# Another order for words 331 to pair 10, and seventeen steps on other engines

## The chip, the cores and the metric

The kernel runs on one core of a Trainium2 chip. A core has five engines that each work through their own list of instructions in order: TensorE (PE, with its weight loads PEld), VectorE (DVE), ScalarE (ACT), GpSimd (POOL) and SyncE (SP), which issues nearly all DMAs here. They meet through semaphores alone. The metric is the device time of one execution in microseconds (us); lower is better.

## The reference

Windowed attention in front of a feed-forward block with a SoLU gate, all in float32, with errors held small enough that the large products are taken in high and low parts:

```
scores = q k^T / 8, masked: heads 0-3 a window of 32, heads 4-7 every 4th of 128 back
attn   = softmax(scores);  x = attn v            8 batches x 576 tokens, 8 heads of 64
h      = x @ w_in                                4608 tokens, 512 -> 1024
solu   = h * softmax(h)
ln     = (solu - mean) / sqrt(var + 1e-6) * g_ln
out    = ln @ w_out                              1024 -> 512
```

## The kernel before

**Work.** Attention goes in 32 units (a batch and two heads); the feed-forward block in 36 tiles of 128 tokens. The order of everything is written out by hand as a list of words: a name and a number is one step of one unit or tile. `OPENING` (line 50) holds the words of the first 26 tiles or so, word for word; behind it `pair_words` (line 137) makes the words for pairs of tiles r = 13 to 17. `run` and the loop at line 1006 call one small function for each word, in order, and each function appends its instructions to the lists of the engines it uses. Nothing is moved afterwards: the order of the words *is* the order on each engine, and an engine that waits holds all that stands behind it on that engine, SP's DMA issues too.

**A unit n.** `S` scores on PE (line 311, 40 matmuls, each recorded as two of 64 columns), `mask` and `max` on DVE (329, 340), `sub` on POOL (353), `exp` on ACT (357), `sum` and `inv` on DVE (361, 367), `norm` on DVE or POOL (372), `turn` on DVE (377: the weights are transposed into `pt`), `V` on PE (406: 80 or 92 small matmuls with `pt`), then `xh`/`xf` on ACT (450, 453) and `xl`/`xd` (464, 471, or a DMA) put x into the tiles x_hi and x_lo.

**A tile i.** Tiles 0 to 11 take `ha` to `hd` on PE (485); from tile 12 on two tiles r = 6, 7, ... share seven block products `P1` to `P7` (844) on sums `z`, `hS`, `lS`, `hA`, `lA` (672, 675, 802, 817), whose results ACT and DVE gather (`s` 862, `c` 868). Then `peak` or `pk` (496, 875) and `gate` (520) on DVE, `e` (511) and `var` (536) on ACT, `mid` (centring: DVE 532, or ACT 529), `forth` and `back` (the tile goes to DRAM and comes back with its rows turned), `trA`/`trB` on DVE (592), `thA`/`thB` on ACT (600: high part), `tlA`/`tlB` on POOL or DVE (606: low part), `o` or `oA`, `oB` on PE (615: 24 or 12 matmuls of 512 columns) and `out` (627).

**Which engine.** Tables by number decide for the steps that either of two engines can do:

```
371  eng = nc.gpsimd if n in POOL_NORM else nc.vector
527  if (i in ACT_CENTRE) != (PAIRED <= i < NTILE - 2):   # then centre on ACT, else on DVE
605  on_pool = i < NTILE - 3 and f"tl{'AB'[c]}{i}" not in ON_DVE
```

So for tiles 12 to 33 a tile named in `ACT_CENTRE` is centred on DVE, and one that is not named on ACT.

Of the kernel before, what the change touches and what calls it, by code (L numbers as in the profile page):

```python
# [37 lines left out]
SIGN_BIT = 1 << 15  # L38
PE_MASK = (0, 1, 2, 3, 4, 5, 6, 7, 8, 9)
POOL_SUB = True  # L40
POOL_NORM = (0, 1, 2, 3, 4, 5, 6, 7, 8, 9, 12, 14, 15, 20, 22)
ACT_SCORES = ()
POOL_X = (2, 4, 5, 6, 9)
DVE_LOW = (0, 4, 8, 9, 10, 11, 12, 14, 15)
ACT_CENTRE = (0, 3, 4, 5, 6, 7, 8, 10, 11, 14, 15, 16, 17, 18, 19)
Q_BUFS, V_BUFS, T_BUFS, TH_BUFS, CONV_BUFS = 4, 4, 4, 2, 4
REBIAS = 2.0**-112
TO_ZERO = 2.0**-100
# [73 lines left out]
)  # L122
PAIR_HEAD = "S.u V.y P1.r trB.c xf.y P2.r trA.c s1.r mask.u thB.c "
# [43 lines left out]
WIDE = ()  # L167
AFTER = {}
SHIFT = {}
ON_DVE = ("tlA2", "tlB2", "tlA4", "tlA6", "fc0", "fb1", "fh0", "fa1", "fd1", "fc1", "tlB7", "fh1", "tlA9", "tlB9", "tlA10", "tlA11", "tlA12", "tlB14", "tlA16", "tlB16", "tlB17", "tlB18", "tlA18", "tlA19", "tlB3", "tlB4", "tlB5", "fd0", "tlA5", "tlA7", "fg1", "tlB10", "tlB11", "tlA13", "tlB13", "tlA14", "tlB19", "fe0", "fg0", "tlA8", "tlB15", "tlA17",)  # L170


@with_exitstack
def windowed_attention_then_solu_kernel(
# [159 lines left out]
    def wide(x):  # L334
        return x.unsqueeze(3).broadcast_to([P, 2, NS, WQ])
# [33 lines left out]
    def soft_norm(n):  # L369
        sm, rs = st[n]["sm"], st[n]["rs"]  # L370
        eng = nc.gpsimd if n in POOL_NORM else nc.vector
        eng.tensor_tensor(out=sm, in0=sm, in1=wide(rs), op=ALU.mult)
# [152 lines left out]
    def moe_centre(i):  # L525
        src, dst, mu = ms[i]["t"], ms[i]["t"], ms[i]["mu"]
        if (i in ACT_CENTRE) != (PAIRED <= i < NTILE - 2):
            nc.vector.tensor_scalar(out=mu, in0=mu, scalar1=-1.0 / DF, scalar2=None, op0=ALU.mult)  # L528
# [29 lines left out]
    def part_of_t(name, i):  # L558
        name = f"{name}{i % TH_BUFS}"
        if name in SHIFT and name not in shifted:  # L560
            shifted.add(name)
            moe.tile([P, SHIFT[name]], F32, name=f"before_{name}", bufs=1)
        return moe.tile([P, FT, P], F32R, name=name, bufs=1)
# [38 lines left out]
    def low_t(i, c):  # L602
        if "tl" not in ms[i]:
            ms[i]["tl"] = part_of_t("tl", i)
        on_pool = i < NTILE - 3 and f"tl{'AB'[c]}{i}" not in ON_DVE
        (nc.gpsimd if on_pool else nc.vector).tensor_tensor(  # L606
# [104 lines left out]
    def sums_engine(word):  # L711
        return nc.vector if word in ON_DVE else nc.gpsimd

# [378 lines left out]
```

## Time and profile before

| | |
|---|---|
| three runs, median | 492.19 us (491.38 to 492.32) |
| the profiled execution, its own time | 491.03 us |
| its span, first to last instruction | 489.2 us |
| granted TensorE clock, mean | 1.000 |
| PE busy | 462.2 us, 94% of the span; 6988 matmuls, each with a weight load |
| DVE, ACT, POOL busy | 358.4, 299.6, 263.1 us |

PE is the engine to read: from 37 us on, the page shows it busy for 90% or more of every fortieth of the span but the last. Matmuls are pipelined, so a long matmul's own duration (390 ns) says little; the distance from one start to the next does.

### The profile page before, as it was taken

How to read it: one execution, taken by the hardware profiler on the slowest of the kernel's cores; microseconds unless marked ns; L12 is line 12 of the kernel's file. 1: busy time of each engine (PE TensorE's matmuls, PEld its weight loads, DVE VectorE, ACT ScalarE, POOL GpSimd, SP SyncE). 2: the span in 40 equal slices, each digit the busy share in tenths (PEclk: the TensorE clock that was granted, in tenths of full speed). 3: DMA queues.
4: the chain of work that ended last, by engine and by line, in shares of the span. 5: the costliest groups of instructions: out<-in, count | busy, mean ns of one | idle time of the engine just before them, and what ended most of it. 6: DMA issues, size and time to landing. Idle time of an engine off the chain costs nothing.

```text
span 489.2 us, 16365 instructions
## 1 busy us (share of the span) xinstructions
PE 462.2 (94%) x6988; PEld 373.9 (76%) x6988; DVE 358.4 (73%) x625; ACT 299.6 (61%) x502; POOL 263.1 (54%) x332
## 2 busy tenths in 40 slices
PE   2559999999999999999999999999999999999997
PEld 1346788888887887878778878888888888888885
DVE  1857999868879796879678997788496754445572
ACT  3769898455653445664555544866486666667552
POOL 0344467535352549958862734466576756766420
PEclk9999999999999999999999999999999999999999
DMA  8887766657743374755676855766755545353462
GB/s 302 343 291 271 236 206 189 199 188 247 246 146 108 121 225 119 237 153 162 226 219 168 253 187 193 211 214 213 254 172 161 165 135 166 98 166 120 121 179 78
DMA packets 50760, 94.05 MB, mean 192 GB/s; under 512 B 5632, under 2 KB 25472, under 8 KB 50688
## 3 DMA queue, kind: packets, MB, share of 16 engines
q1 hardware_dynamic: 49968, 92.37, 60.0%
q8 instruction: 54, 0.88, 0.8%
q10 hardware_dynamic: 720, 0.66, 0.4%
q14 instruction: 18, 0.15, 0.1%
HBM read 59.97 MB, written 28.31 MB: 180 GB/s over the span
## 4 chain that ended last, share of the span: by engine, by line
PE 78%; DVE 10%; POOL 4%; ACT 3%; issue 3%; DMA 1%; SPq 0%; DVEq 0%; ACTq 0%; POOLq 0%
PE banks L615 32%; PE banks L844 21%; PE banks L485 10%; PE banks L406 6%; PE banks L311 5%; PE banks L650 2%; DVE mx L340 1%; DVE t L592 1%; DMA packed<-pack 1%; DVE t L520 1%; PE banks L303 1%; DVE low L672 1%; DVE sm L350 1%; DVE tl L606 1%; DVE pt L377 1%
## 5 line engine op out<-in xcount | busy, mean ns | idle before, releaser
L615 PE MATMUL banks<-w_o,th 128*128 128x512 f32 x544 | 169.1, 392 | 0.0
L615 PEld LDWEIGHTS banks<-w_o,th 128*128 128x128 f32 x544 | 101.3, 188 | 21.7 <-DVE w_o L943 0.4
L615 PE MATMUL banks<-w_o,tl 128*128 128x512 f32 x272 | 106.2, 390 | 1.2 <-DVE tl L606 1.2
L606 POOL TENSOR_TENSOR tl<-t,th 128x512 fp32r<-128x512 f32 x35 | 47.1, 1353 | 42.1 <-ACT th L600 42.1
L485 PE MATMUL banks<-w_i,x_hi 128*128 128x512 f32 x192 | 62.1, 405 | 0.0
L615 PEld LDWEIGHTS banks<-w_o,tl 128*128 128x128 f32 x272 | 51.1, 188 | 12.6 <-DVE tl L606 2.0
L600 ACT CAST th<-t 128x512 fp32r<-128x512 f32 x68 | 41.0, 618 | 22.5 <-DVE t L592 19.0
L868 DVE CUSTOM_DVE_ANT_0 t<-banks,t 128x512 f32<-128x512 f32 x36 | 24.5, 682 | 37.3 <-PE banks L844 29.0
L406 PEld LDWEIGHTS banks<-pt,vt 32*64 32x64 f32 x2752 | 35.0, 140 | 14.7 <-issue 8.1
L592 DVE STREAM_TRANSPOSE t<-raw 128x512 f32<-128x512 f32 x68 | 45.3, 689 | 0.5 <-DMA raw<-mid 0.5
L406 PE MATMUL banks<-pt,vt 32*64 32x64 f32 (+3 forms) x2752 | 38.5, 236 | 6.9 <-issue 4.7
L353 POOL TENSOR_TENSOR sm<-sm,mx 128x640 f32<-128x640 f32 x22 | 29.2, 1328 | 28.4 <-DVE mx L340 28.4
L485 PEld LDWEIGHTS banks<-w_i,x_hi 128*128 128x128 f32 x192 | 35.3, 190 | 7.6
L511 ACT ACTIVATE e<-t,nmax 128x1024 f32<-128x1024 f32 x23 | 26.5, 1152 | 22.8 <-DVE nmax L875 22.6
L311 PEld LDWEIGHTS banks<-kt,qt 64*32 64x32 f32 x2560 | 29.5, 110 | 14.2 <-issue 11.4
L627 ACT ACTIVATE ob<-banks,rstd 128x512 f32<-128x512 f32 x35 | 24.0, 686 | 26.0 <-PE banks L615 17.5
L529 ACT ACTIVATE t<-t,mu 128x1024 f32<-128x1024 f32 x25 | 28.8, 1153 | 18.1 <-DVE mu L528 17.6
L536 ACT ACTIVATE e<-t 128x1024 f32<-128x1024 f32 x35 | 37.0, 1056 | 4.3 <-DVE t L532 4.1
L311 PE MATMUL banks<-kt,qt 64*32 64x64 f32 x2560 | 35.5, 235 | 3.5 <-issue 3.5
L485 PE MATMUL banks<-w_i,x_lo 128*128 128x512 f32 x96 | 38.1, 397 | 0.1
L606 DVE TENSOR_TENSOR tl<-t,th 128x512 fp32r<-128x512 f32 x37 | 30.6, 842 | 8.3 <-ACT th L600 6.7
L862 ACT COPY t<-banks 128x512 f32<-128x512 f32 x36 | 21.1, 587 | 24.1 <-PE banks L844 21.2
(161 smaller groups left out, 937.4 us busy)
## 6 DMA issues: line engine op xcount, KB each, us to landing
mid<-t SPq DMA_DIRECT2D x140, 128.0 KB, 2.7
raw<-mid SPq DMA_DIRECT2D x34, 512.0 KB, 4.1
vt<-vw SPq DMA_DIRECT2D x32, 384.0 KB, 4.4
kt<-kT SPq DMA_DIRECT2D x32, 312.0 KB, 4.8
qt<-qT SPq DMA_DIRECT2D x32, 296.0 KB, 5.2
out<-ob SPq DMA_DIRECT2D x35, 256.0 KB, 2.7
x_hi<-x SPq DMA_DIRECT2D x12, 288.0 KB, 3.9
t<-w_in SPq DMA_DIRECT2D x5, 512.0 KB, 6.5
```

The source lines that it names most:

```text
L311: nc.tensor.matmul(out=ps[WIN * c : WIN * c + WIN, h, WQ * i : WQ * i + WQ], lhsT=qt[D * h : D * h + D, q0 : q0 + WIN], rhs=kt[D * h : D * ...
L353: eng.tensor_tensor(out=st[n]["sm"], in0=st[n]["sm"], in1=wide(mx), op=ALU.subtract)
L406: nc.tensor.matmul(out=ps_x[D * h : D * h + D, c, c0 : c0 + k1 - k0], lhsT=vt[WIN * c : WIN * c + WIN, i, D * h : D * h + D], rhs=pt[WIN * ...
L485: nc.tensor.matmul(out=ps_h(i)[:, half], lhsT=a[:, kt, xs], rhs=w_i[:, kt, half, part, :], start=(kt == 0 and k == 0), stop=(kt == KT - 1 ...
L511: nc.scalar.activation(out=e, in_=h, func=AF.Exp, bias=nmax, scale=1.0, accum_out=se)
L529: nc.scalar.activation(out=dst, in_=src, func=AF.Identity, bias=mu, scale=1.0)
L536: nc.scalar.activation(out=e, in_=t, func=AF.Square, accum_out=per_tile(i, "sq"))
L592: nc.vector.transpose(out=turned(i)[:, cut(c)].rearrange("p k (a r) -> p k a r", r=WIN), in_=ms[i]["mv"].rearrange("p (a k s) -> p k a s", ...
L600: nc.scalar.copy(out=ms[i]["th"][:, cut(c)], in_=turned(i)[:, cut(c)])
L606: (nc.gpsimd if on_pool else nc.vector).tensor_tensor(out=ms[i]["tl"][:, cut(c)], in0=turned(i)[:, cut(c)], in1=ms[i]["th"][:, cut(c)].bit ...
L615: nc.tensor.matmul(out=ps_o(i), lhsT=a[:, f, :], rhs=w_o[:, f, part, :], start=(f == 0 and k == 0), stop=(f == FT - 1 and k == 2), skip_gr ...
L844: nc.tensor.matmul(out=banks[:, bank], lhsT=left(pa, kt), rhs=right(pb, kt), start=j in (1, 2, 5) and kt == 0 and k == 0, stop=kt == 1 and ...
```

## The change

It replaces the middle of `OPENING` from word 331 (`S11`, `mask11`, ...) to where the sums of pair 11 are ready (680 words, the same ones in another order; the 330 before and the 497 behind are untouched). The new order comes from a planner that asks for half a microsecond between the end of a step and its use by TensorE. Three tables change with it:

- `POOL_NORM`: units 10, 11, 21, 23, 25 move their `norm` from DVE to POOL, unit 20 from POOL to DVE.
- `ACT_CENTRE`: tiles 9, 16, 17, 18, 19 move their `mid` from DVE to ACT, tiles 6, 8, 20, 21 from ACT to DVE.
- `ON_DVE`: `tlA3` and `tlB6` move from POOL to DVE.

```
-POOL_NORM = (0, 1, 2, 3, 4, 5, 6, 7, 8, 9, 12, 14, 15, 20, 22)
+POOL_NORM = (0, 1, 2, 3, 4, 5, 6, 7, 8, 9, 10, 11, 12, 14, 15, 21, 22, 23, 25)
-ACT_CENTRE = (0, 3, 4, 5, 6, 7, 8, 10, 11, 14, 15, 16, 17, 18, 19)
+ACT_CENTRE = (0, 3, 4, 5, 7, 9, 10, 11, 14, 15, 20, 21)
...
-    "trB2 trA2 back3 out1 e5 gate5 thA2 hc6 mid5 trB3 back4 ha6 S11 mask11 out0 xh8 tlA2 thB2 "
+    "trB2 trA2 back3 out1 e5 gate5 thA2 hc6 mid5 trB3 back4 ha6 var5 thB2 tlA2 max10 q12 S11 "
...
-ON_DVE = (..., "tlB15", "tlA17",)
+ON_DVE = (..., "tlB15", "tlA17", "tlA3", "tlB6",)
```

On PE the words of the stretch stand, before and now (the bars enclose runs of small attention matmuls):

```
before  |S11| hd6 hb6 o2 ha7 hb7 |V9 S12| hc7 hd7 o3 |V10 S13| ha8 hc8 hd8 hb8 o4 |S14 V11| ha9 hc9 o5
        hb9 hd9 |S15 V12| o6 ha10 hb10 hc10 hd10 o7 ha11 |V13 S16| hc11 hb11 |V14| hd11 o8 |V15| o9 P1.6
        |S17| P2.6 P5.6 P6.6 P3.6 P7.6 |S18| P4.6 P2.7 oA10 P1.7 P5.7 oB10 |S19 V16| P6.7 P3.7 P7.7 oA11
        |S20 V17| P4.7 oB11 P2.8 |V18| P1.8 oA12 P6.8 P5.8 |V19| oB12 P7.8 P3.8 |S21| oA13 oB13 |S22| oA14
        P4.8 oB14 P1.9 P5.9 |S23 V20| P2.9 P6.9 P3.9 oA15 P7.9 |S24 V21| P4.9 oB15 P5.10 P1.10 oA16 P2.10
        oB16 |V22 S25| oA17 oB17 P6.10 P3.10 |V23| P7.10 oA18 oB18 P4.10 oA19 oB19
now     |S11| hd6 hb6 |S12| o2 |V9| ha7 hb7 hc7 hd7 |V10 S13| o3 ha8 hc8 hd8 hb8 o4 |V11 S14| hc9 o5
        hd9 ha9 hb9 o6 |S15 V12| hc10 ha10 hb10 hd10 |S16| o7 ha11 |V13| hc11 hd11 |V14| o8 |V15| hb11 o9
        P1.6 |S17| P5.6 P6.6 P2.6 |S18| P3.6 P7.6 oA10 P4.6 oB10 P1.7 P5.7 |V16| P2.7 P6.7 |S19| P3.7 P7.7
        |V17 S20| P4.7 oA11 oB11 P1.8 P2.8 P5.8 |V18 S21| oA12 P6.8 oB12 P7.8 P3.8 |V19| oA13 oB13 |S22|
        P4.8 oA14 |S23 V20| oB14 P1.9 P2.9 P5.9 P6.9 P3.9 P7.9 oA15 oB15 P4.9 P2.10 |S24 V21| P1.10 P5.10
        oA16 oB16 |V22 S25| P6.10 oA17 |V23| P3.10 oB17 P7.10 oA18 oB18 P4.10 oA19 oB19
```

Three places in the built programs (names carry the buffer's number and a running number; the running numbers differ between the two programs). First VectorE ahead of `V15`; `x_lo` is `xl14`, `pt1` is `turn15`. Before:

```order
L471 TENSOR_TENSOR x_lo_89<-banks_90,x_hi_88 128x576
L672 TENSOR_TENSOR mag3_2835<-vt2_2097,more_2361 128x512
L672 TENSOR_TENSOR mag1_2837<-qt3_1807,tp_2120 128x512
L592 STREAM_TRANSPOSE t1_2497<-raw5_2586 128x512
L329 TENSOR_TENSOR sm0_93<-banks_90,packed_83 128x10x64
L340 TENSOR_REDUCE mx_2872<-sm0_93 128x10
L606 TENSOR_TENSOR tl1_2878<-t1_2497,th1_2843 128x512
L377 STREAM_TRANSPOSE pt1_2880<-sm1_94 128x640
```

Now:

```order
L672 TENSOR_TENSOR kt3_1808<-kt3_1808,vt2_1995 128x512
L471 TENSOR_TENSOR x_lo_89<-banks_90,x_hi_88 128x576
L329 TENSOR_TENSOR sm0_93<-banks_90,packed_83 128x10x64
L340 TENSOR_REDUCE mx_2821<-sm0_93 128x10
L471 TENSOR_TENSOR x_lo_89<-banks_90,x_hi_88 128x576
L377 STREAM_TRANSPOSE pt1_2830<-sm1_94 128x640
L606 TENSOR_TENSOR tl1_2834<-t1_2483,th1_2776 128x512
L592 STREAM_TRANSPOSE t1_2483<-raw5_2748 128x512
```

Between `xl14` and `turn15` stood six steps, and none stands there now.

Second, VectorE ahead of `oA17`; `tl1` is the low part that `oA17` reads, `mx` with `sm0` the maximum of unit 24, `sm1` unit 23. Before (the double row at `tl1` is `tlA17` and `tlB17`):

```order
L672 TENSOR_TENSOR vt2_3877<-x_hi_88,vt2_3877 128x256
L531 TENSOR_SCALAR mu_4389<-mu_4389 128x1
L532 TENSOR_SCALAR t3_4136<-t3_4136,mu_4389 128x1024
L361 TENSOR_REDUCE rs_4399<-sm1_94 128x10
L592 STREAM_TRANSPOSE t1_3737<-raw5_4285 128x512 x2
L340 TENSOR_REDUCE mx_4420<-sm0_93 128x10
L592 STREAM_TRANSPOSE t2_4064<-raw4_4375 128x512
L367 RECIPROCAL rs_4399<-rs_4399 128x10
L606 TENSOR_TENSOR tl1_4483<-t1_3737,th1_4402 128x512 x2
```

Now (the first row is `tlA17`, and the second `tl1` row `tlB17`; `mx_4383` is again unit 24):

```order
L606 TENSOR_TENSOR tl1_4251<-t1_3774,th1_4219 128x512
L868 ISA t3_4142,m2_4339<-banks_90,zero_98 128x512
L868 ISA m2_4339 128x1
L875 TENSOR_SCALAR nmax_4341<-m1_4190,m2_4339 128x1
L606 TENSOR_TENSOR tl0_4237<-t0_3718,th0_4152 128x512
L340 TENSOR_REDUCE mx_4365<-sm1_94 128x10
L520 ISA t3_4142,mu_4367<-t3_4142,e_4350 128x1024
L520 ISA mu_4367 128x1
L329 TENSOR_TENSOR sm0_93<-banks_90,packed_83 128x10x64
L340 TENSOR_REDUCE mx_4383<-sm0_93 128x10
L528 TENSOR_SCALAR mu_4367<-mu_4367 128x1
```

`tlA17` stood behind the sum of unit 23 and the maximum of unit 24, and now stands ahead of the gate of tile 19 and of both maxima.

Third, TensorE at `S16` (the row of line 311); before it follows `V13` (the four rows of line 406) in one run of small matmuls:

```order
L485 MATMUL banks_90<-w_i_86,x_hi_88 128x512 x2
L485 MATMUL banks_90<-w_i_86,x_lo_89 128x512
L406 MATMUL banks_90<-pt1_2556,vt1_2177 64x32 x6
L406 MATMUL banks_90<-pt1_2556,vt1_2177 64x64 x24
L406 MATMUL banks_90<-pt1_2556,vt1_2177 64x48 x8
L406 MATMUL banks_90<-pt1_2556,vt1_2177 64x16 x8
L311 MATMUL banks_90<-kt0_2352,qt0_2351 32x64 x40
L485 MATMUL banks_90<-w_i_86,x_hi_88 128x512 x2
```

Now:

```order
L485 MATMUL banks_90<-w_i_86,x_hi_88 128x512 x2
L485 MATMUL banks_90<-w_i_86,x_lo_89 128x512
L311 MATMUL banks_90<-kt0_2383,qt0_2382 32x64 x40
L615 MATMUL banks_90<-w_o_87,th1_2377 128x512 x2
L615 MATMUL banks_90<-w_o_87,tl1_2380 128x512
```

`S16` has become a run of its own between products of 512 columns.

## Rows read from the trace of the kernel before

**Rows 1.** Windows: length, busy PE, PEld, DVE, ACT, POOL, PE clock, DMA share, GB/s.
```profile
100.69:316.59 215.90, 213.11 (x3339) 172.95 (x3339) 177.70 (x294) 119.05 (x201) 121.90 (x154) 1.00 0.61 190
```
**Rows 2.** The two longest waits of PE there: total us, times, longest us.
```profile
PE banks L615 <- DVE tl L606: 1.2, 2, 0.6
PE banks L406 <- DVE pt L377: 0.8, 1, 0.8
```
**Rows 3.** Timeline of PE at `S11`: start us, us, instructions.
```profile
99.92 0.62 PE L485 MATMUL banks<-w_i,x_hi 128*128 128x512 f32 x2
100.37 0.39 PE L485 MATMUL banks<-w_i,x_lo 128*128 128x512 f32 x1
100.69 1.04 PE L311 MATMUL banks<-kt,qt 64*32 64x64 f32 x80
101.66 0.73 PE L485 MATMUL banks<-w_i,x_hi 128*128 128x512 f32 x2
102.23 0.40 PE L485 MATMUL banks<-w_i,x_lo 128*128 128x512 f32 x1
```
**Rows 4.** Timeline of PE: the end of `o8`, and `V15`.
```profile
183.13 0.39 PE L615 MATMUL banks<-w_o,tl 128*128 128x512 f32 x1
184.29 1.08 PE L406 MATMUL banks<-pt,vt 32*64 32x64 f32 x80 [0.77 <-DVE pt L377]
```
**Rows 5.** Timeline of PE: `V12`.
```profile
150.36 0.83 PE L406 MATMUL banks<-pt,vt 32*64 32x32 f32 x56
151.92 0.64 PE L406 MATMUL banks<-pt,vt 32*64 32x64 f32 x36 [0.72 <-issue]
```
**Rows 6.** Timeline of PE: the first matmuls of `oB10`.
```profile
210.11 0.40 PE L615 MATMUL banks<-w_o,th 128*128 128x512 f32 x1
211.09 0.51 PE L615 MATMUL banks<-w_o,tl 128*128 128x512 f32 x1 [0.58 <-DVE tl L606]
211.43 0.40 PE L615 MATMUL banks<-w_o,th 128*128 128x512 f32 x1
```
**Rows 7.** Timeline of PE: the first matmuls of `oA17`.
```profile
291.49 0.73 PE L615 MATMUL banks<-w_o,th 128*128 128x512 f32 x2
292.81 0.50 PE L615 MATMUL banks<-w_o,tl 128*128 128x512 f32 x1 [0.58 <-DVE tl L606]
```
**Rows 8.** Timeline of PE: second and third matmul of `P7.8`.
```profile
242.80 0.39 PE L844 MATMUL banks<-low,w_i 128*128 128x512 f32 x1
243.23 0.50 PE L844 MATMUL banks<-qt,w_i 128*128 128x512 f32 x1
```
**Rows 9.** DMA queues of the page: packets, MB, share of 16 engines.
```profile
q8 instruction: 54, 0.88, 0.8%
```
**Rows 10.** Timeline at 285 us: `gate19` and `lA2.10` on DVE, `sub23` on POOL.
```profile
285.36 1.23 DVE L520 CUSTOM_DVE_ANT_0 t<-t,e 128x1024 f32<-128x1024 f32 x1
...
286.51 1.47 DVE L672 TENSOR_TENSOR vt<-x_hi,vt 128x256 fp32r<-128x256 f32 x1
...
285.40 2.31 POOL L353 TENSOR_TENSOR sm<-sm,mx 128x640 f32<-128x640 f32 x1 [3.34 <-DVE mx L340]
```
**Rows 11.** `sub` on POOL, all 22: duration ns min/median/max.
```profile
L353 POOL TENSOR_TENSOR sm<-sm,mx x22: 1260/1264/2309, 107.3 to 383.5; 128x640 f32<-128x640 f32 x22
```
**Rows 12.** Groups by line: count, busy us, mean ns, idle before.
```profile
L372 DVE TENSOR_TENSOR sm<-sm,rs 128x640 f32<-128x640 f32 x17 | 15.4, 911 | 0.3
L372 POOL TENSOR_TENSOR sm<-sm,rs 128x640 f32<-128x640 f32 x15 | 19.4, 1294 | 30.4 <-DVE rs L367 28.7 <-ACT ob L627 1.6
L532 DVE TENSOR_SCALAR t<-t,mu 128x1024 f32<-128x1024 f32 x11 | 10.6, 965 | 0.4
L529 ACT ACTIVATE t<-t,mu 128x1024 f32<-128x1024 f32 x25 | 28.8, 1153 | 18.1 <-DVE mu L528 17.6 <-POOL tl L606 0.5
L606 DVE TENSOR_TENSOR tl<-t,th 128x512 fp32r<-128x512 f32 x37 | 30.6, 842 | 8.3 <-ACT th L600 6.7 <-issue 1.0 <-ACT th L642 0.7
L606 POOL TENSOR_TENSOR tl<-t,th 128x512 fp32r<-128x512 f32 x35 | 47.1, 1353 | 42.1 <-ACT th L600 42.1
```

More of the change, by code (lines that the diff above doesn't have):

```diff
@@ L169 @@
 SHIFT = {}
-ON_DVE = ("tlA2", "tlB2", "tlA4", "tlA6", "fc0", "fb1", "fh0", "fa1", "fd1", "fc1", "tlB7", "fh1", "tlA9", "tlB9", "tlA10", "tlA11", "tlA12", "tlB14", "tlA16", "tlB16", "tlB17", "tlB18", "tlA18", "tlA19", "tlB3", "tlB4", "tlB5", "fd0", "tlA5", "tlA7", "fg1", "tlB10", "tlB11", "tlA13", "tlB13", "tlA14", "tlB19", "fe0", "fg0", "tlA8", "tlB15", "tlA17",)
+ON_DVE = ("tlA2", "tlB2", "tlA4", "tlA6", "fc0", "fb1", "fh0", "fa1", "fd1", "fc1", "tlB7", "fh1", "tlA9", "tlB9", "tlA10", "tlA11", "tlA12", "tlB14", "tlA16", "tlB16", "tlB17", "tlB18", "tlA18", "tlA19", "tlB3", "tlB4", "tlB5", "fd0", "tlA5", "tlA7", "fg1", "tlB10", "tlB11", "tlA13", "tlB13", "tlA14", "tlB19", "fe0", "fg0", "tlA8", "tlB15", "tlA17", "tlA3", "tlB6",)
 @with_exitstack
```

104 rows, old and new, of the table OPENING are left out of this document.

## The prediction

> **What bounds the kernel now.** I read the windows first. In the changed stretch, 215.90 us long, TensorE is busy for 213.11, at a granted clock of 1.00, which is the 2.4 GHz level; VectorE has 177.70, GpSimd 121.90, ScalarE 119.05 [rows 1]. So TensorE bounds the stretch, its work is the same before and after, and no order can save more than the time in which it issues nothing or issues late. The idle time alone is 215.90 - 213.11 = 2.8 us. PE's waits put names to most of it: 1.2 us in two waits for a low part, 0.8 for a transposed `pt` [rows 2], and 0.72 in the middle of `V12` under "issue", where no semaphore is seen [rows 5].
>
> The busy time hides more, because a matmul is booked with its latency. The distances between starts show it. Inside `ha6` two matmuls take 100.37 - 99.92 = 0.45 us, so 0.227 each; a run of small matmuls starts 0.32 behind the last wide one (0.09 more than the pitch), and behind it the first two wide ones take 102.23 - 101.66 = 0.57, 0.12 more [rows 3]. Each run of attention matmuls so costs 0.2 us for being apart from the others, whatever waits.
>
> **What the waits cost, one by one.** Read from starts, with the pitches just given:
>
> - `V15`: from `o8`'s last matmul to its first, 184.29 - 183.13 = 1.16 instead of 0.32: 0.84 [rows 4]. It waited for `turn15`.
> - `V12`: 56 small matmuls from 150.36, which at `S11`'s rate (0.97 us for 80 [rows 3]) take 0.68; the next starts at 151.92: 0.88 lost, with no producer named [rows 5].
> - `oB10`: 211.09 - 210.11 = 0.98 instead of 0.227, and the one behind starts 0.34 later, 0.11 over the pitch (the price of a restart): 0.86 [rows 6].
> - `oA17`: 292.81 - 291.49 = 1.32 where two matmuls behind small ones take 0.57: 0.75 [rows 7].
> - `P7.8`: 0.43 instead of 0.227, and a restart: 0.31 [rows 8]. Two more products (`P5.7`, `P6.8`) show the restart alone: 0.22.
>
> Together 3.86 us. That is what the new order can give back at most.
>
> **The change, part by part.** *Waits removed.* `turn15`: before, six VectorE steps stand between `xl14` and `turn15`; now none does. `V14`, `xl14` and `turn15` follow each other while `o8`'s 24 matmuls run, 24 x 0.227 = 5.4 us, and a VectorE step of this size takes about 0.9 us [rows 12]. What is late next there is the chain from `V15` to `P5.6` (x copied, `z1`, `z2`, `z4`, `lS12` on GpSimd), which has `hb11`, `o9`, `P1.6` and `S17` beside it; that is as much cover as before. `tlA17`: now ahead of `gate19` and both maxima, and five products (`oA16` and `oB16` among them) and two runs of attention stand between that point of the list and `oA17`; it has several us to spare. `tlB10` stood on VectorE behind `gate13` and now stands ahead of `norm16` and of everything that VectorE does for pair 6. I take these stalls, and those at `P7.8`, `P5.7` and `P6.8`, as gone at their old places (the last three I did not count out); what comes in their stead is the unknown below.
>
> `V12`: the 54 packets of the instruction queue hold 0.88 MB [rows 9], 16 KB each; PE has 13,976 matmuls and weight loads, about 256 to a packet. `S15` and `V12` are 172 small matmuls, 344 instructions, issued within 2 us: here one whole packet lies inside small matmuls, and I read the wait as the next one's arrival. Counted in the new order, only the run `V22 S25` still holds a whole packet, and it did before, without a wait. I take the 0.88 as gone; if it stays, the sum is 0.9 higher.
>
> The Trainium skill speaks against this reading: "Runtime: NRT & Kernel Launch", section "Instruction fetch mechanics", says that fetching is hidden because instructions are dispatched slower than they are filled in. By that rule the wait has another cause and may come back, and the sum would be 1.6 us instead of 2.5. The trace has an "issue" wait with no producer in the middle of `V12`, which is nearer to the fetch.
>
> *Runs added.* `V9 S12`, `V13 S16` and `S19 V16` are split, and `V18` and `S21` are joined; 20 runs become 22. Two more at 0.2 us: +0.4. It could be 0 if the split runs stand where PE waits anyway, and 0.45 by the pitches above.
>
> *Steps on other engines.* Norms: net four fewer on VectorE (4 x 0.91 = 3.6 us) and four more on GpSimd (4 x 1.29 = 5.2). Centrings: five leave VectorE and four come (0.97 against 1.15 on ScalarE, net about 1 us). Low parts: two more on VectorE (1.7 us), two fewer on GpSimd (2.7) [rows 12]. VectorE ends some 3 us lighter of 178, GpSimd 2.5 heavier of 122. None of this is on TensorE's path; the cover is the 0.5 us planned ahead of each use. If the cover fails, a step costs what it is late, plus 0.11.
>
> *Waits added.* This is the unknown part. A step that uses two inputs in SBUF on GpSimd can be stretched by one on VectorE: `sub23` took 2.31 us beside `gate19`, where the median is 1.26 [rows 10, 11], so 1.05 late, and `lA2.10`, which stood ahead of `tlA17` on VectorE, took 1.47 beside `sub23`. Half a microsecond covers half of the 1.05: 1.05 - 0.5 + 0.11 = 0.66 for each use that is hit. Of the waits above, those at `oB10`, `oA17` and `P7.8` have such a step in their chain. If as many are hit again, and half of these stand where only the planned 0.5 is spare, 1.5 x 0.66 = 1.0 us comes back. The bounds: 0 (no use is hit; below 0 is excluded, since PE can't go under its pitch) and 3.9, all that was lost before. I take 1.0, nearer to the lower end, because the waits were of 0.6 to 0.8 us and the spare of 0.5 is most of that.
>
> "SBUF — State Buffer", section "Who interferes with whom" of the Trainium skill, has a stricter form: of a GpSimd step and a VectorE step with two SBUF inputs, the later waits for the whole of the earlier. `sub23` agrees: the gate's 1.23 us and then its own 1.26 from 285.36 end at 287.85, and it ended at 287.71. By that rule the four norms that go to GpSimd raise the number of such meetings; what this would do is the third rival below.
>
> **Sum.** -3.86 + 0.40 + 1.0 = -2.5 us. The profiled execution would go from 491.03 to 488.5; the median of the runs stands 1.16 above that execution, so 492.19 becomes **489.7 us**.
>
> **Rivals.** *All the spare holds.* No use is late: -3.86 + 0.4 = -3.5, 488.7 us. For it: the waits shown are all under 0.9 us. Against it: single steps are stretched by more than 0.5.
>
> *The waits only move.* The spare is a plan's and not a measured one; the old order, too, was written out with every step ahead of its use, and lost 3.86. If new uses lose as much less the 0.4 of the runs, say 3.5, the time stays at 492.2. For it: VectorE is busy for 82% of the stretch. Against it: the old waits stand where the producer was within 0.1 us of its use or behind it, and most uses with half a us were not hit.
>
> *GpSimd's queue is late (slower).* In pairs 7 to 10, `z1` to `z4`, `lS12`, `lS34`, `sub` and now the norms of units 21, 23 and 25 follow each other on GpSimd, and each waits for the one before. If two steps of such a chain are each stretched by 1.05, a product loses 2 x 1.05 - 0.5 + 0.11 = 1.7; with one in each of three pairs, 5.1 us, and the sum is -3.86 + 0.4 + 5.1 = +1.6: 493.8 us. It decides from the point where GpSimd's products wait in three of the four pairs. For it: norms with two SBUF inputs are 1.29 us long there instead of 0.91. Against it: GpSimd is busy for 56% of the stretch, and the products of these pairs have several PE words between.
>
> **How the numbers follow.** The forecast (1 to 3.4 us faster) has a chance of 0.50, all spare held 0.15, waits only moved 0.19, GpSimd late 0.16. About 0.2%, 1 us, is what a measurement of this kernel can tell from no change. Faster: 0.50 + 0.15 and a little of the third, 0.66. Same: 0.18. Slower: the last, 0.16. The likeliest case by itself spans 488.8 to 491.2. For eight in ten, the low end is the best case less the half us by which runs differ, 488.2; the high end takes in the moved waits and half of the slow case, 492.9.
>
> **What would show it.** Right: in the changed stretch PE's idle time falls from 2.8 to under 1 us, no wait of PE over 0.5, no "issue" wait in `V12`, `turn15` done well before `o8` ends, and 22 runs of small matmuls with the same 0.2 each. Wrong: PE waits for `w_i` (line 672) on GpSimd, `sm` (372) ahead of a transposition, or an "issue" wait at another run; or the stretch is shorter, and the unchanged words behind it wait for what PE now reaches earlier.

## The result, and the profile after

The changed kernel takes 487.83 us in the median of 6 runs (486.95 to 488.08) against 492.25 of the kernel before on the same chip: a ratio of 0.9905, 95% interval 0.9888 to 0.9923. Faster was right; the time lies 1.9 us below the 489.7 forecast and 0.4 below the range. The profiled execution took 487.35 us (span 485.3), 3.68 less than that of before.

From the start of `S11` to the end of `S26`, in the columns of [rows 1]:

```profile
100.52:312.64 212.12, 212.09 (x3340) 172.93 (x3339) 172.05 (x291) 119.49 (x202) 121.53 (x154) 1.00 0.62 191
```

The stretch takes 212.12 us instead of 215.90, so 3.78 less, and PE idles for 0.03 us of it, not for 2.8. The view of PE's waits, which named three in [rows 2] and the one in `V12`, has no row left. In the groups by line (columns as in [rows 12]) the low part has no idle time ahead of it, where it had 1.2:

```profile
L615 PE MATMUL banks<-w_o,tl 128*128 128x512 f32 x272 | 105.9, 389 | 0.0
```

The places of [rows 4 to 7] in the timeline of PE (start us, us, instructions), first `o8` and `V15` (the view's window ends inside `V15`), then `V12`, `oB10` and `oA17`:

```profile
181.19 0.39 PE L615 MATMUL banks<-w_o,tl 128*128 128x512 f32 x1
181.51 0.72 PE L406 MATMUL banks<-pt,vt 32*64 32x64 f32 x44
...
155.97 1.16 PE L406 MATMUL banks<-pt,vt 32*64 32x32 f32 x92
157.06 0.50 PE L485 MATMUL banks<-w_i,x_hi 128*128 128x512 f32 x1
...
204.16 0.61 PE L615 MATMUL banks<-w_o,th 128*128 128x512 f32 x2
204.61 0.39 PE L615 MATMUL banks<-w_o,tl 128*128 128x512 f32 x1
...
289.86 0.61 PE L615 MATMUL banks<-w_o,th 128*128 128x512 f32 x2
290.31 0.39 PE L615 MATMUL banks<-w_o,tl 128*128 128x512 f32 x1
```

`V15` starts 0.32 behind `o8`'s last matmul, where it had started 1.16 behind it, and `turn15` now ends 2.5 us ahead of `V15` (0.05 before); all 92 matmuls of `V12` are one row; in `oB10` and `oA17` two matmuls take 0.45, the plain pitch. The prices of a run of small matmuls are where they were, at `S16` as at `S11` in [rows 3]: 0.31 on entry, 0.58 for the first two wide ones behind.

```profile
162.41 0.39 PE L485 MATMUL banks<-w_i,x_lo 128*128 128x512 f32 x1
162.72 1.04 PE L311 MATMUL banks<-kt,qt 64*32 64x64 f32 x80
163.69 0.74 PE L615 MATMUL banks<-w_o,th 128*128 128x512 f32 x2
164.27 0.40 PE L615 MATMUL banks<-w_o,tl 128*128 128x512 f32 x1
```

What did not change is how far steps of VectorE and GpSimd stretch. `sub` (the answer to [rows 11]), and two groups by line that answer to [rows 12]:

```profile
L353 POOL TENSOR_TENSOR sm<-sm,mx x22: 1261/1264/2305, 101.7 to 379.6; 128x640 f32<-128x640 f32 x22
...
L372 POOL TENSOR_TENSOR sm<-sm,rs 128x640 f32<-128x640 f32 x19 | 24.6, 1293 | 35.7 <-DVE rs L367 35.6
L372 DVE TENSOR_TENSOR sm<-sm,rs 128x640 f32<-128x640 f32 x13 | 12.6, 972 | 0.3
```

So the meetings that the prediction feared still happen, and in this trace no use is late for them.

### The profile page after: what moved, and what is told of

It reads as the page before. It is cut to its first block, busy times and chain, and to the rows that moved or that the text cites. A ratio compares the mean times of both kernels' runs of the same rounds, so it can differ in the third digit from the quotient of the medians.

```text
span 485.3 us, 16380 instructions
## 1 busy us (share of the span) xinstructions
PE 461.1 (95%) x6988; PEld 374.1 (77%) x6988; DVE 352.4 (73%) x622; ACT 300.4 (62%) x503; POOL 264.5 (54%) x334
## 4 chain that ended last, share of the span: by engine, by line
PE 93%; DVE 2%; issue 2%; DMA 1%; ACT 1%; SPq 0%; ACTq 0%
PE banks L615 39%; PE banks L844 24%; PE banks L485 14%; PE banks L406 7%; PE banks L311 6%; PE banks L650 2%; DMA packed<-pack 1%; PE banks L303 1%; DVE sm L350 1%; DVE mx L340 1%; ACT w_i L933 0%; SPq L251 0%; DVE mag L922 0%; ACT x_hi L453 0%; DVE w_i L941 0%
## 5 line engine op out<-in xcount | busy, mean ns | idle before, releaser
L606 POOL TENSOR_TENSOR tl<-t,th 128x512 fp32r<-128x512 f32 x33 | 43.0, 1312 | 32.3 <-ACT th L600 32.3
L372 POOL TENSOR_TENSOR sm<-sm,rs 128x640 f32<-128x640 f32 x19 | 24.6, 1293 | 35.7 <-DVE rs L367 35.6
L529 ACT ACTIVATE t<-t,mu 128x1024 f32<-128x1024 f32 x26 | 30.0, 1153 | 21.9 <-DVE mu L528 21.4
L353 POOL TENSOR_TENSOR sm<-sm,mx 128x640 f32<-128x640 f32 x22 | 30.5, 1389 | 19.4 <-DVE mx L340 12.9
```

Of the source, the lines that this page charges most:

```text
L353: eng.tensor_tensor(out=st[n]["sm"], in0=st[n]["sm"], in1=wide(mx), op=ALU.subtract)
L529: nc.scalar.activation(out=dst, in_=src, func=AF.Identity, bias=mu, scale=1.0)
L606: (nc.gpsimd if on_pool else nc.vector).tensor_tensor(out=ms[i]["tl"][:, cut(c)], in0=turned(i)[:, cut(c)], in1=ms[i]["th"][:, cut(c)].bit ...
```

## The experiments

Each kernel ran beside the kernel before on one chip, whose median there is given with the ratio. Where a stretch is given, it goes from the start of `S11` to the start of `S26`: 214.93 us before, 211.16 after. In e3 and e4 the list of words takes two lines fewer, so line numbers there are two lower.

### Order or tables

**e1_order_only** is the new order with the three old tables; **e2_tables_only** the old order with the three new ones.

```
e1: POOL_NORM, ACT_CENTRE, ON_DVE as before; OPENING as after
e2: POOL_NORM, ACT_CENTRE, ON_DVE as after;  OPENING as before
```

> The changed kernel's order of words with the three tables of before (the seventeen small steps stay on the engines that had them). Theory 'the spare holds' (the order alone takes the waits away, since each use stands behind its producer with time to spare): 487.8 to 489.0 us, at least 3.2 of the 4.4 us between the two kernels; TensorE waits under 1 us in all between S11 and S26. Rival 'the tables carry it' (without the steps on other engines the queues run late and TensorE waits again): 490.5 to 492.5, with waits on lA, c or s of VectorE and GpSimd that add up to 2.5 us or more.

Measured: 488.43 us, ratio 0.9917 (0.9895 to 0.9939; before 492.07). The stretch takes 211.33, and PE's waits have no row. The order alone carries all but 0.2 us of the stretch.

> The order of before with the three tables of the changed kernel. Theory 'the spare holds': the uses stand as tight as before, so 491.5 to 493.0 us (within 0.8 us of before), with lost time still at V15, V12, oB10 and oA17. Rival 'the tables carry it': 489 to 490.5, two or three of these four waits gone.

Measured: 499.12 us, ratio 1.0126 (1.0101 to 1.0152). Both theories missed: the tables alone cost 7 us in the medians, and the stretch grows by 5.4 us, to 220.36. PE's four largest waits (us in total, times, longest):

```profile
PE banks L844 <- ACT t L862: 2.5, 2, 2.2
PE banks L615 <- DVE tl L606: 1.4, 3, 0.6
PE banks L406 <- issue: 1.2, 1, 1.2
PE banks L844 <- DVE m L868: 0.8, 1, 0.8
```

The longest, at `P3.9`, is followed back in two rows: `s5.9` on ScalarE waits for `tlA15` on GpSimd, and on GpSimd `tlA15` (the second row) stands behind `norm21`, which the new table put there and which waited for VectorE's `inv21`:

```profile
271.18 0.59 ACT L862 COPY t<-banks 128x512 f32<-128x512 f32 x1 [2.77 <-POOL tl L606]
...
268.65 1.26 POOL L372 TENSOR_TENSOR sm<-sm,rs 128x640 f32<-128x640 f32 x1 [10.19 <-DVE rs L367]
269.88 1.27 POOL L606 TENSOR_TENSOR tl<-t,th 128x512 fp32r<-128x512 f32 x1
```

GpSimd had nothing to do for 10 us and still was late: an engine in order waits with all that stands behind. This is the queue of the third rival, in the old order, but held by an input that came late and not by stretched steps. It accounts for 2.2 us, the wait at `P3.9`; the rest of the loss lies at other places, `P4.10` and the packet waits of `V12` and `S16` among them. In the new order `norm21` waits 0.75 us for `inv21`, not 10.19, and the same tables cost nothing.

### Removing the waits in place

**e8_four_moves** and **e4_five_moves** take the kernel before and move only the late producers; e4 has a fifth move.

```
-"... max16 sub16 exp16 v16 tlA9 turn15 peak11 ..."       +"... max16 turn15 sub16 exp16 v16 tlA9 peak11 ..."
-"... turn16 mask18 gate13 ... hS34.7 tlB10 P5.7 ..."     +"... turn16 tlB10 mask18 gate13 ... hS34.7 P5.7 ..."
-"... trB17 max24 trA18 ... thA18 tlA17 ..."              +"... trB17 tlA17 max24 trA18 ... thA18 ..."
-"... mask14 S15 ... sub14 V12 e9 ... o6 ha10 ..."        +"... mask14 ... sub14 e9 ... o6 S15 V12 ha10 ..."
e4 also:
-"... q22 e15 c11.8 turn19 z3.8 ... sub20 hS34.8 ..."     +"... q22 hS34.8 e15 c11.8 turn19 z3.8 ... sub20 ..."
```

> The kernel before with five short moves and nothing else: turn15 is put right behind max16, tlB10 ahead of mask18 and gate13, tlA17 behind trB17, hS34.8 ahead of e15, and S15 V12 behind o6. Theory 'the five losses add' (each of V15 0.84, V12 0.88, oB10 0.86, oA17 0.75, P7.8 0.31 is a loss of its own): 3.4 to 3.6 us faster than before, 488.6 to 489.0. Rival 'waits only move' (a step that came just in time behind the wait is late once the wait is gone: P5.6, S18 and P5.7 stand with under 0.2 us of spare): half or less of it, 490.4 to 491.5, with new waits at those places.

Measured: 494.84 us, ratio 1.0056 (1.0034 to 1.0078): slower, which neither theory gave. The fifth move was a mistake. `z3.8` overwrites the tile that `hS34.8` reads, so it had to wait for it. (`hS34.8` ahead of it takes the high part of what the tile holds from the pair before; the low part makes up the difference.) GpSimd's idle time ahead of `z3.8`, and PE's waits:

```profile
238.07 0.74 POOL L670 TENSOR_TENSOR kt<-x_hi 128x256 f32<-128x256 f32 x1 [3.51 <-ACT w_i L800]
...
PE banks L842 <- POOL w_i L670: 3.8, 3, 3.0
PE banks L613 <- ACT ob L625: 0.9, 1, 0.9
PE banks L842 <- DVE m L866: 0.4, 1, 0.4
PE banks L309 <- issue: 0.4, 1, 0.4
```

> The kernel before with four moves: turn15 right behind max16, tlB10 ahead of mask18 and gate13, tlA17 behind trB17, S15 V12 behind o6. It is e4 without hS34.8 ahead of e15, which had made GpSimd's z3.8 wait 3.5 us (z3.8 overwrites what hS34.8 reads). Theory 'the losses add': 0.84 + 0.88 + 0.86 + 0.75 = 3.3 us faster than before. Rival 'waits only move' (as seen in e4: P5.6 0.5, P5.7 0.6, the bank of out16 at oA17 1.1, S16 0.5, P4.10 0.6): 0.3 to 1.0 us faster than before.

Measured: 490.97 us, ratio 0.9972 (0.9953 to 0.9991; before 492.02): 1.1 us faster in the medians, 0.2 shorter in the traced stretch (214.76), both well under the 3.3 of "the losses add". The four places run through, and PE waits elsewhere:

```profile
PE banks L615 <- ACT ob L627: 0.9, 1, 0.9
PE banks L311 <- DMA qt<-qT: 0.6, 1, 0.6
PE banks L844 <- DVE m L868: 0.5, 1, 0.5
PE banks L311 <- issue: 0.3, 1, 0.3
PE banks L844 <- POOL w_i L672: 0.3, 1, 0.3
```

These rows add up to 2.6 us, those of before to 2.7. "Waits only move" holds for local moves: `oA17` has its low part in time and now waits for the bank that `out16` frees, `S18` for the load of `q18`, `P4.10` for `c22.10`.

**e11_second_round** goes one round further.

```
-"... o9 out9 P1.6 ... pk12 q18 S18 ..."     +"... o9 q18 out9 P1.6 ... pk12 S18 ..."
-"... trA17 thA17 oB16 out16 trB17 ..."      +"... trA17 oB16 out16 thA17 trB17 ..."
```

> e8 with two of the waits that it showed taken out in place: q18 loaded ahead of out9 (S18 lost 0.81) and out16 ahead of thA17 (oA17 lost 1.07). Theory 'waits only move': tlA17, now later on ScalarE's and VectorE's way, is late for oA17 again (0.3 to 0.7 us), c22.10 too, and of the 1.9 us some 0.8 to 1.2 are kept: 489.7 to 490.3. Rival 'the losses add': 489.0 to 489.2.

Measured: 490.98 us, ratio 0.9966 (0.9945 to 0.9985; before 493.06); stretch 214.47, so 0.3 of the 1.9 us was kept, less than either theory. `oA17` now waits 0.3 for `thA17`, `P5.6` and `P5.7` 0.5 each for `lS12` on GpSimd. (In before, `lS12.6` had ended 0.51 us ahead of its use and `lS12.7` 0.06.)

### The packets of instructions

**e3_packet_shift** is the fourth of the moves above alone; **e5_packet_back** and **e12_packet_again** the reverse in the changed kernel.

```
e5, e12 (after): -"... peak9 o6 S15 turn13 ... V12 out5 ..."   +"... peak9 S15 turn13 ... V12 o6 out5 ..."
```

> The kernel before with the two words S15 V12 put behind o6 instead of ahead of it: the same runs, but the 256 TensorE instructions that came as one instruction packet at 149.3 us now fall into two that each take in some 512-column products. Theory 'instruction packet': the 0.72 us wait marked issue inside V12 goes, and the pitch through o6, S15 and V12 adds up to 0.8 to 0.9 us less; 491.3 us, if nothing later takes it back. Rival 'a wait inside V12 for data' or 'no packet': the same 0.7 us stay, wherever V12 stands; 492.2.

Measured: 490.92 us, ratio 0.9982 (0.9962 to 1.0003; before 492.07), which the times alone can't tell from no change. The trace can: `V12`'s wait is gone, although its data and `S15`'s were ready in both orders. What it gave came back as 0.9 at `oA17` (`out16`) and a 0.3 "issue" wait inside `S16`, behind its 49th small matmul of 80, where the next packet boundary falls.

> The changed kernel with o6 put behind V12 instead of ahead of S15, so that again one whole instruction packet (144 instructions of S15 and 112 of V12) lies in the small matmuls; all data are ready several us ahead in both orders. Theory 'instruction packet': a wait marked issue of 0.2 to 1.2 us appears at the 57th matmul of V12 and TensorE's time from S11 to S26 grows by 0.3 to 1.3 us: 488.2 to 489.1. Rival 'no packet': V12 runs through as in the changed kernel, 487.8.

> e5 a second time, for one more trace of V12 with a whole packet in S15 V12. If the wait marked issue depends on the execution (how busy the DMA engines are when the packet is fetched), it may show this time, 0.2 to 1.2 us at the 57th matmul of V12; if it depends on the kernel's order alone, V12 runs through again.

Measured: 488.01 us, ratio 0.9902 (0.9870 to 0.9934), and 488.19 in the single run. `V12` runs through in both traces, so a whole packet inside small matmuls isn't enough for a wait. (In the trace of before it cost nothing either in `V13 S16`, `S19 V16` and `V22 S25`.) What is missing came from e7.

**e7_five_merged** joins five runs of small matmuls to their neighbours in the changed kernel.

```
-"... v10 sub11 S12 fa0 ... o2 xl8 V9 ..."             +"... v10 sub11 fa0 ... o2 xl8 S12 V9 ..."
-"... peak10 out6 ff1 e10 S16 o7 ... xl12 V13 ..."     +"... e10 o7 ... xl12 S16 V13 ..."
-"... V15 xf15 ... thA10 S17 q19 ..."                  +"... V15 S17 xf15 ... thA10 q19 ..."
-"... V16 v18 ... trA12 S19 P3.7 ..."                  +"... V16 S19 v18 ... trA12 P3.7 ..."
-"... V19 forth15 ... xd19 S22 z1.9 ..."               +"... V19 S22 forth15 ... xd19 z1.9 ..."
```

> The changed kernel with five scores moved beside another run of small matmuls: S12 ahead of V9, S16 ahead of V13, S17 behind V15, S19 behind V16, S22 behind V19; 17 runs instead of 22 between S11 and S26, all inputs ready. Theory 'a run costs 0.2': 5 x 0.2 = 1.0 us less, 486.8. Theory 'instruction packet' beside it: three packets of 256 now lie whole in S12 V9, S16 V13 and V16 S19, which gives waits marked issue of 0.2 to 0.9 us each: the 1.0 is eaten up, 487.2 to 489.0, with the waits at the boundary inside these three runs and none in V15 S17 and V19 S22.

Measured: 493.68 us, ratio 1.0018 (0.9997 to 1.0038): the whole gain of the change is lost in the medians, more than either theory had. Not all of it is waiting: ten of the twelve executions have a mean granted TensorE clock of 0.996 or 0.997 and take 492.46 to 494.87 us, the two at 1.000, the traced one and another, 491.09 and 491.24. Against the changed kernel's 487.83 that is 5.9 us in the median and 3.3 at the full clock; where the clock falls in the ten no trace shows. In the trace, nearly all that PE waits for is "issue", at `V9` (0.34), `V13` (1.64), `S19` (0.56) and, unforeseen, in `oA13` behind `V19 S22` (1.33), where 249 of the 256 are small:

```profile
PE banks L406 <- issue: 2.0, 2, 1.6
PE banks L615 <- issue: 1.3, 1, 1.3
PE banks L311 <- issue: 0.6, 1, 0.6
PE banks L311 <- DMA qt<-qT: 0.2, 1, 0.2
```

In the timeline, `S16` and `V13`; 132 instructions of `S16` and 124 of `V13`, 62 matmuls, are the packet:

```profile
169.86 1.04 PE L311 MATMUL banks<-kt,qt 64*32 64x64 f32 x80
170.83 0.87 PE L406 MATMUL banks<-pt,vt 32*64 32x32 f32 x62
173.33 0.44 PE L406 MATMUL banks<-pt,vt 32*64 32x48 f32 x30 [1.64 <-issue]
```

The DMA view of the window 170.98 to 171.94 holds one transfer, a packet of instructions, and that of 171.95 to 173.30, most of the wait, none at all:

```profile
DMA packets 1, 0.02 MB, mean 17 GB/s; under 512 B 0, under 2 KB 0, under 8 KB 0
q8 instruction: 1, 0.02, 6.2%
...
DMA packets 0, 0.00 MB, mean 0 GB/s; under 512 B 0, under 2 KB 0, under 8 KB 0
```

So the packet has landed at 171.94 and PE goes on at 173.33, 1.39 later. At ten such waits (in before, e2, e7, e8, e10 and e11) the DMA records give 1.24 to 1.66 us from the end of that transfer to the restart. Whether other transfers run meanwhile makes no visible difference: there were none in four of the ten (1.36 to 1.54 us), and 12 to 158 in the others. A packet that is all small matmuls lasts 1.5 us, so what counts is how far behind the packet's start the next one's transfer ends: 0.07 ahead in e5, 0.20 behind in e12 and 0.26 in before's `S16`, with no wait; 0.34 behind in e11's `S16`, a wait of 0.02 us; 0.64 in e8's, 0.30; 1.23 in before's `V12`, 0.72; 1.96 in `V13` here, 1.64. When a transfer begins (from 3.2 us ahead of the packet to 1.3 behind its start) no run here explains.

### The spare itself

**e6_three_late** takes the changed kernel and puts three steps later.

```
-"... gate17 mid17 lA1.9 P1.9 ... inv21 ... trA15 ..."    +"... gate17 mid17 inv21 trA15 lA1.9 P1.9 ..."
-"... mid18 c22.9 oA15 hA1.10 trA17 ..."                  +"... mid18 trA17 c22.9 oA15 hA1.10 ..."
-"... S24 V21 c21.9 ... P1.10 tlB16 ..."                  +"... S24 V21 tlB16 c21.9 ... P1.10 ..."
```

> The changed kernel with three steps of VectorE put one or two places later: lA1.9 behind inv21 and trA15 (0.85 us later; it ended 0.31 us ahead of its first matmul in P1.9), c22.9 behind trA17 (0.70 later; 0.57 ahead of P4.9), c21.9 behind tlB16 (0.69 later; 0.08 ahead of P1.10). Theory 'a use waits for what its spare lacks, plus 0.11 for the restart': P1.9 loses 0.5 to 0.7, P4.9 0.1 to 0.3, P1.10 0.6 to 0.8 us: 1.2 to 1.8 us in all, 489.0 to 489.6. Rival 'something behind the spare takes it up' (the chain of waits moves as a whole, or VectorE was waiting there anyway): under 0.5 us in all, 487.8 to 488.3.

Measured: 489.34 us, ratio 0.9928 (0.9901 to 0.9954): 1.5 above the changed kernel, of which the stretch shows 0.8 (211.95). `P1.10` loses 0.57, just under what was expected, and `P4.9` 0.17 and a restart of 0.1, as expected. `V21` and `P1.10`, first in the changed kernel, then in e6:

```profile
276.90 1.16 PE L406 MATMUL banks<-pt,vt 32*64 32x32 f32 x92
278.00 0.96 PE L844 MATMUL banks<-w_i,x_lo 128*128 128x512 f32 x3
```
```profile
278.02 1.16 PE L406 MATMUL banks<-pt,vt 32*64 32x32 f32 x92
279.68 1.20 PE L844 MATMUL banks<-w_i,x_lo 128*128 128x512 f32 x4 [0.50 <-DVE m L868]
```

`P1.9` loses nothing: `lA1.9` lasts 0.86 instead of 1.55. The rows are `lA1.9` and GpSimd's `sub22`, first in the changed kernel, then in e6:

```profile
258.11 1.55 DVE L672 TENSOR_TENSOR x_lo<-x_hi,x_lo 128x512 fp32r<-128x512 f32 x1
...
256.80 2.31 POOL L353 TENSOR_TENSOR sm<-sm,mx 128x640 f32<-128x640 f32 x1
```
```profile
259.67 0.86 DVE L672 TENSOR_TENSOR x_lo<-x_hi,x_lo 128x512 fp32r<-128x512 f32 x1
...
257.67 2.31 POOL L353 TENSOR_TENSOR sm<-sm,mx 128x640 f32<-128x640 f32 x1
```

In both, `lA1.9` ends 0.55 us behind the end of `sub22`, begun early or late: started 1.0 us ahead of that end it is stretched to 1.55, started 0.3 ahead to 0.86. So a start 0.76 us later against that of `P1.9` ended only 0.07 later. In e1, where it starts 0.47 behind the end of `sub22`, `lA1.9` takes 0.68.

### Once more, and a version with fewer runs

**e9_after_again** is the changed kernel unaltered; **e10_two_merged** joins `S17` to `V15` and `S22` to `V19`, with `q17` earlier and `P3.8` behind the run.

```
-"... sub16 forth10 ... tlA9 q17 Th3 ... V15 xf15 ... S17 q19 ..."
+"... sub16 q17 forth10 ... tlA9 Th3 ... V15 S17 xf15 ... q19 ..."
-"... c22.8 P3.8 c12.8 pk16 v20 V19 ... trB14 oB13 norm20 trA14 xd19 S22 ..."
+"... c22.8 v20 V19 S22 trB14 P3.8 norm20 trA14 c12.8 pk16 ... oB13 xd19 ..."
```

> The changed kernel once more, beside e10 and many runs of the kernel before on one chip. Theory 'the spare also takes up what differs between executions': its times lie within 1.5 us of each other while those of before spread over 3 us or more, 487.2 to 488.3 in the median, and TensorE again waits under 0.1 us between S11 and S26. Rival 'one lucky trace': waits of 0.3 us or more at P1.9, P1.10 or P2.10 (0.08 to 0.3 us of spare), and a spread like that of before.

Measured: 487.42 us, ratio 0.9896 (0.9865 to 0.9927; before 493.06). PE's waits have again no row and the stretch takes 210.81, so the trace was no lucky one. The spread was missed: 486.49 to 489.66, 3.2 us, where before has 4.3 in 17 runs (2.6 without the seven whose mean granted clock is 0.997 or lower; in e9 none is). Part of it lies ahead of the change: `S11` starts between 100.0 and 101.8 us in the traces of this study, in kernels whose words are alike up to a few ahead of it.

> The changed kernel with two runs of small matmuls fewer: S17 right behind V15 (with q17 loaded ahead of forth10, since its load came just in time in e7) and S22 right behind V19 (with P3.8, trB14, norm20 and trA14 put so that no packet of 256 lies whole in the run; e7 lost 1.3 us there). Theory 'a run costs 0.2 us and nothing else changes': S11 to S26 takes 0.4 us less than in e9, 487.4 against 487.8, no new wait. Rival 'the spare behind is used up': a wait of 0.3 us or more at P3.6, oA13 or P4.8, and no gain.

Measured: 487.62 us, ratio 0.9900 (0.9869 to 0.9932): no difference from e9 in the medians; the stretch is 0.4 longer, 211.20. The two merges save their 0.4; `oA13` loses 0.38 to a packet wait, though only 239 of its packet's instructions are small, and `P1.9` 0.29 and a restart of 0.11 to `lA1.9`, as the rival had it in kind. At `oA13`:

```profile
245.05 0.61 PE L615 MATMUL banks<-w_o,th 128*128 128x512 f32 x2
245.88 0.39 PE L615 MATMUL banks<-w_o,tl 128*128 128x512 f32 x1 [0.22 <-issue]
```

No version beat the changed kernel.

## Why the prediction was right or wrong

- **The bound and the waits.** Right: PE bounds the stretch, and the five stalls were what could be had. The removed sum was a little too small: -3.86 + 0.40 = -3.46 foretold 0.22 less than the 3.68 by which the profiled executions differ. Left out were `S18`'s wait for its load (0.16) and the restart behind `oA17` (0.11).
- **"Waits added", +1.0: the step that failed.** It measured 0 in after and e9, and in e1 two losses, 0.21 at `P3.9` and 0.24 at `P4.9` with their restarts. The argument took a stretched step (1.05) to come on top of a spare of 0.5. But such a stretch recurs at the same place (`sub22` takes 2.29 to 2.31 in all eight traces of the new order), and what the trace shows as spare is what is left with it. Left it is by little: `c21.9` ends 0.08 us ahead of `P1.10`, `lA1.10` 0.18 ahead of `P2.10`, `lA1.9` 0.31 ahead of its first use in `P1.9`. e6 shows that this spare is real and has no second cushion behind it: `c21.9`, 0.69 later, costs 0.57 there. The bound 0 was the truth, and I held it for the less likely.
- **"All the spare holds"**, the rival at 0.15, is what happened. It too was 0.9 too high, for the offset from the profiled execution to the median: 1.16 before, taken over as it was; it is 0.48 after. Of the error of 1.9 us, 1.0 is the added waits, 0.2 the removed sum and 0.7 this offset, which the prediction took as fixed. It need not be free of the order: of the 62 executions of before that stand beside the experiments, 14 have a mean granted TensorE clock of 0.997 or lower and take 494.15 us in the median, the 46 at 0.999 or higher 491.97; of the 33 of the changed kernel, e1, e5, e6, e9, e10 and e12 none is below 0.998. No trace caught such an execution, so what brings the clock down, and whether the removed waits do, stays open.
- **"Waits only move"** is right for local moves (e8, e11) and wrong for the whole order. It was argued that the old order, too, had each step ahead of its use. The runs show the difference: there, uses behind a removed wait had little spare (0.06 us at `lS12.7`), so they were late once the wait was gone; in the new order all got enough.
- **"GpSimd's queue late"** did not come in the new order. e2 shows such a queue, held by a late input and not by two stretched steps, in a wait of PE of 2.2 us; the tables cost 7 us there in all and are harmless only in the order made for them. The prediction read the steps on other engines as load (VectorE 3 us lighter, GpSimd 2.5 heavier; in the stretch they came out 5.7 and 0.4 lighter), and load was not what decided; the place in the queue was.
- **Steps and runs.** 22 runs at 0.2 each: right. The reading of `V12` as an instruction packet: right, shown by e3 (gone when the boundary moved) and e7 (made at will). The Trainium skill ("Runtime: NRT & Kernel Launch", section "Instruction fetch mechanics") has fetching hidden behind slower dispatch; at most places the traces agree, and where a whole packet of small matmuls is issued in 1.5 us they can fail to: in e7's `V13` PE waited 1.64 us with no other DMA under way. That the whole packet is enough, as the prediction counted, is wrong: in `V22 S25`, e5 and e12 it cost nothing.
- **Contention.** "SBUF — State Buffer", section "Who interferes with whom", of the Trainium skill lets the later of two such steps wait for the earlier. By it `lA1.9` would end its own 0.68 us (what it took in e1) behind the end of `sub22`; it ended 0.54 to 0.56 behind in all seven traces where the two overlap. The rule holds within 0.15 us. In after, e6 and e9 PE lost nothing by it; in e5, e7 and e10, where `P1.9` came sooner, it lost 0.2 to 0.4 us to `lA1.9`, restart included, the kind of loss that the prediction feared.

## What to carry to other kernels

Where the bounding engine loses a little at many places, removing the losses one by one moves them; ask for every use at once, with a spare, and expect little of the spare to be left and still to suffice. A table of which engine does what has no value of its own: the same tables cost 7 us in one order and nothing in another. Before joining small matmuls to save a switch of 0.2 us, count where 256 instructions of them fall together, since one such place can cost eight times that.

## What was not expected of the hardware

At ten waits PE restarted 1.24 to 1.66 us after the transfer of its next 16 KB instruction packet had ended, with the DMA engines idle meanwhile or not. And a step put later can end hardly later: `lA1.9` took 0.86 us instead of 1.55, and its end stayed 0.55 behind that of GpSimd's `sub22`.
